# Ending a kernel in more and smaller output tiles: the third token tile in two parts, the fourth in three, stores on two queues in turn

## The chip, the cores and the metric

The kernel runs on one core of one Trainium2 chip. Its time is device time in microseconds (us). Every execution quoted here was in the fast state, with TensorE's granted clock at 1.0 (0.999 in one of e7's). A comparison counts as faster or slower only when it is clear of 2%, which is 32 us here.

TensorE (PE) multiplies matrices, VectorE (DVE) does the additions, ScalarE (ACT) and SyncE (SP) issue the stores, and 16 DMA engines move the data. Engines and DMAs tell each other that something is done by counters called semaphores, and an instruction can wait for them. An accumulator is what the matmuls of one part write (`dacc` and `dacc_pair` in the traces), called a bank; in the code below `pair` is one tile made of two of them.

## The reference

```python
x = x + A(layernorm(x), wqkv, wo)                # attention over 8 positions, 2 apart
x = x + B(layernorm(x), W_gate, W_up, W_down)    # h = relu(x @ W_gate) * (x @ W_up); h @ W_down
x = x + A(layernorm(x), wqkv, wo)
x = x + B(layernorm(x), W_gate, W_up, W_down)
# x: 2048 tokens x 1024 columns, bf16; hidden width 3584
```

The change concerns only the last thing that the kernel does: the product with `W_down` for the last block of 512 tokens, for the second half (512) of the 1024 columns. Its result is added to x and stored. The 512 tokens are four tiles of 128, called t0 to t3 below. The hidden width gives 28 contraction steps of 128.

## The kernel before

```python
def cols_of(half):                               # the parts in which a half is accumulated
    cols = [(t, 0, SLAB) for t in range(TPB)]    # four token tiles, 512 columns each
    if n == NN - 1 and half == 1:                # the very last half: t3 in two parts
        cols[-1:] = [(TPB - 1, 0, SLAB // 2), (TPB - 1, SLAB // 2, SLAB)]
    return cols

def mults(half, s8):                             # 8 of the 28 steps (4 in the last call)
    ...
    if half == 1:
        pair = psum_l.tile([P, TPB // 2, BLK], F32, tag="L", name="dacc_pair")   # two banks, one tile
        own = {2: pair[:, 0, :], 3: pair[:, 1, :]} if len(cols) == TPB else {2: pair[:, 0, :]}
    accs[half] = [own[i] if i in own else psum.tile([P, BLK], F32, tag="acc", ...)[:] for i in range(len(cols))]
    ...
    for a, (t, c0, c1) in zip(accs[half], cols):
        for jl in range(nfc):
            mm(a[:, c0:c1], lhsT=hT[:, j, t * P:(t + 1) * P], rhs=wsl[:, jl, c0:c1], ...)

def adds(half):
    for a, (t, c0, c1) in zip(accs[half], cols_of(half)):
        run(nc.vector.tensor_tensor, xs, a[:, c0:c1], xs, op=ALU.add)
        if n == NN - 1:
            if half == 1 and t % 2 == 1 and c0 == 0:
                nc.scalar.dma_start(dst, xs)     # ScalarE's queue
            else:
                sp_dma(dst, xs)                  # SyncE's queue
...
def store_x(n):                                  # stores of the three blocks ahead of the last
    for t in range((n % NB) * TPB, (n % NB + 1) * TPB):
        sp_dma(out_dram[t * P:(t + 1) * P, :], x_tiles[t][:])
```

An output part goes through four steps: its matmuls in the four last steps of the contraction, its addition on VectorE, the issue of its store, the store's landing. After that come SyncE's five closing waits, each for two semaphores.

## Time and profile before

| | before |
|---|---|
| time, median of 3 runs | 1618.47 us (1617.82 to 1618.52) |
| span of the profiled run | 1616.7 us |
| PE busy | 1611.1 us |
| last matmul ends / last add ends | 1613.57 / 1614.09 us |
| last store issued / landed | 1614.12 / 1615.68 us |

The page's engines and its chain that ended last (each step followed back to what released it) of the kernel before:

```profile
PE 1611.1 (100%) x7633; PEld 786.4 (49%) x7633; DVE 1137.4 (70%) x960; ACT 475.5 (29%) x967; POOL 180.9 (11%) x168
PE 99%; DMA 1%; DVE 0%; POOL 0%; issue 0%; DVEq 0%
```

TensorE has no slack, so the rest of the kernel can't hide anything for the end. What can be gained lies behind the last matmul.

The timeline of that end, kernel before. The columns are start in us, length in us, engine, line, operation, what it writes and reads, and, in brackets, idle time before it and what ended it. SPq and ACTq are issues of DMAs by those engines:

```profile
1611.01 0.69 DVE L831 TENSOR_TENSOR x<-dacc,x 128x512 bf16<-128x512 f32 x1 [20.95 <-PE dacc L132]
1611.67 1.03 PE L132 MATMUL dacc_pair<-w_d,hT 128*128 128x512 bf16 x4
1611.73 2.72 SPq L121 DMA_DIRECT2D out_dram<-x  x3
1611.87 0.69 DVE L831 TENSOR_TENSOR x<-dacc,x 128x512 bf16<-128x512 f32 x1 [0.17 <-PE dacc L132]
1612.54 1.04 PE L132 MATMUL dacc<-w_d,hT 128*128 128x256 bf16 x8
1612.60 1.55 ACTq L841 DMA_DIRECT2D out_dram<-x  x2
1612.74 0.69 DVE L831 TENSOR_TENSOR x<-dacc_pair,x 128x512 bf16<-128x512 f32 x1 [0.17 <-PE dacc_pair L132]
1613.34 0.75 DVE L831 TENSOR_TENSOR x<-dacc,x 128x256 bf16<-128x256 f32 x2
```

Each of the adds of t0, t1 and t2 waits for TensorE. The two adds of t3 follow without a wait, so VectorE sets the end there.

The same place one block earlier, kernel before, where t2 and t3 use both banks of the pair (timeline of VectorE):

```profile
1465.91 0.69 DVE L831 TENSOR_TENSOR x<-dacc,x 128x512 bf16<-128x512 f32 x1 [20.89 <-PE dacc L132]
1466.77 0.69 DVE L831 TENSOR_TENSOR x<-dacc,x 128x512 bf16<-128x512 f32 x1 [0.17 <-PE dacc L132]
1468.50 1.29 DVE L831 TENSOR_TENSOR x<-dacc_pair,x 128x512 bf16<-128x512 f32 x2 [1.04 <-PE dacc_pair L132]
```

Here VectorE sits idle for 1.04 us, until the matmuls of *both* banks are done, and then adds both at once. So here the two accumulators of one tile are released together.

### The profile page before, as it was taken

To read this page: it belongs to the slowest core of one execution; us is meant where nothing else is said; L and a number is where in the kernel's file an instruction comes from. 1 tells how busy PE (TensorE), PEld (TensorE's weight loads), DVE (VectorE), ACT (ScalarE), POOL (GpSimd) and SP (SyncE) were. 2 spreads that over 40 slices of the span, in tenths; PEclk is the share of its full clock that TensorE was granted. 3 is DMA by queue.
4 is the path that set the end of the run, shared out by engine and by line. 5 is a ranking of instruction groups with operands and counts; after the bars stand their busy time and mean duration, and the time that the engine had idled before them with its cause. 6 is when DMAs were issued, how large, how long until landed. Compare 5 with 4: busy or idle time off the path is not lost.

```text
span 1616.7 us, 18929 instructions
## 1 busy us (share of the span) xinstructions
PE 1611.1 (100%) x7633; PEld 786.4 (49%) x7633; DVE 1137.4 (70%) x960; ACT 475.5 (29%) x967; POOL 180.9 (11%) x168
## 2 busy tenths in 40 slices
PE   9999999999999999999999999999999999999999
PEld 6646544444444445444454444544445444444444
DVE  5999979996989698929489293893939939311211
ACT  5753312131116313603136031360313311131110
POOL 2400100010003002300053000530005100000000
PEclk9999999999999999999999999999999999999999
DMA  9868868697669766794747947479574884755452
GB/s 302 186 187 242 222 158 261 183 215 204 209 190 220 199 183 213 191 247 149 223 159 204 239 152 228 154 202 256 160 230 153 209 240 156 209 161 177 157 167 67
DMA packets 407448, 317.92 MB, mean 197 GB/s; under 512 B 166464, under 2 KB 387008, under 8 KB 406848
## 3 DMA queue, kind: packets, MB, share of 16 engines
q1 hardware_dynamic: 406784, 316.13, 69.5%
q8 instruction: 59, 0.97, 0.2%
q10 hardware_dynamic: 576, 0.59, 0.1%
q14 instruction: 29, 0.24, 0.0%
HBM read 266.29 MB, written 34.66 MB: 186 GB/s over the span
## 4 chain that ended last, share of the span: by engine, by line
PE 99%; DMA 1%; DVE 0%; POOL 0%; issue 0%; DVEq 0%
PE acc_u L132 24%; PE acc_g L132 24%; PE dacc L132 18%; PE acc_wo L132 7%; PE acc_q L132 7%; PE acc_k L132 7%; PE acc_v L132 7%; PE dacc_pair L132 6%; DMA w_u<-in_B_W_up_dram 0%; DMA x<-in_A_x_dram 0%; POOL rstd L328 0%; DVE xn_first L106 0%; DVE bst L106 0%; PE tp_pair L383 0%; DVE bst L103 0%
## 5 line engine op out<-in xcount | busy, mean ns | idle before, releaser
L132 PE MATMUL acc_u<-xnT_b,w_u 128*128 128x512 bf16 x1792 | 423.3, 379 | 0.1
L132 PE MATMUL acc_g<-xnT_b,w_g 128*128 128x512 bf16 x1792 | 423.3, 379 | 0.0
L784 ACT ACTIVATE r<-acc_g 128x512 bf16<-128x512 f32 x224 | 133.6, 596 | 725.4 <-PE acc_g L132 699.4
L106 DVE TENSOR_TENSOR hT<-acc_u,r 128x512 bf16<-128x512 f32 x224 | 151.3, 690 | 240.6 <-PE acc_u L132 238.2
L132 PE MATMUL dacc<-w_d,hT 128*128 128x512 bf16 (+1 forms) x1400 | 301.9, 375 | 0.0
L132 PEld LDWEIGHTS <-hT 128*128 128x128 bf16 x1820 | 178.1, 98 | 209.0
L132 PEld LDWEIGHTS <-w_u 128*128 128x128 bf16 x1792 | 175.3, 98 | 211.7 <-DMA w_u<-in_B_W_up_dram 0.6
L132 PEld LDWEIGHTS <-w_g 128*128 128x128 bf16 x1792 | 175.3, 98 | 211.4
L106 DVE TENSOR_TENSOR pv<-a,vhm 128x4096 bf16<-128x4096 bf16 x64 | 143.7, 2290 | 0.0
L831 DVE TENSOR_TENSOR x<-dacc,x 128x512 bf16<-128x512 f32 (+1 forms) x38 | 24.5, 673 | 154.1 <-PE dacc L132 154.1
L602 DVE TENSOR_TENSOR t<-q,k 128x2048 f32<-128x2048 bf16 x56 | 128.1, 2293 | 6.7 <-ACT k L537 4.6
L106 DVE TENSOR_TENSOR t<-q,k 128x2048 f32<-128x2048 bf16 x56 | 127.6, 2290 | 3.7 <-ACT k L537 2.6
L106 DVE TENSOR_TENSOR pv<-pv 128x1024 bf16<-128x1024 bf16 (+1 forms) x128 | 113.9, 957 | 0.0
L543 POOL COPY kh<-k 128x14 bf16<-128x14 bf16 x40 | 56.0, 1405 | 504.4 <-ACT k L537 504.4
L132 PE MATMUL acc_wo<-w_o,oT 128*128 128x512 bf16 x512 | 112.0, 379 | 0.0
L615 DVE TENSOR_TENSOR ac<-ac,t 128x2048 f32<-128x2048 f32 x48 | 109.7, 2286 | 0.3
L106 DVE TENSOR_TENSOR ac<-ac,t 128x2048 f32<-128x2048 f32 x48 | 109.8, 2288 | 0.0
L264 POOL TENSOR_TENSOR st_b<-st_b,neg_half 128x1 f32<-128x1 f32 x29 | 43.9, 1521 | 526.2 <-ACT st_b L263 526.2
L132 PE MATMUL dacc_pair<-w_d,hT 128*128 128x512 bf16 x420 | 95.9, 379 | 0.0
L132 PEld LDWEIGHTS <-oT 128*128 128x128 bf16 x512 | 50.1, 98 | 60.6 <-DMA w_o<-in_A_wo_dram 0.5
L259 ACT ACTIVATE xn_b<-x 128x1024 bf16<-128x1024 bf16 x29 | 30.3, 1045 | 128.4 <-DVE x L106 66.3
L441 ACT CAST vT<-acc_v 128x512 bf16<-128x512 f32 x56 | 32.7, 586 | 57.7 <-PE acc_v L132 56.7
(134 smaller groups left out, 1230.1 us busy)
## 6 DMA issues: line engine op xcount, KB each, us to landing
w_g<-in_B_W_gate_dram SPq DMA_DIRECT2D x56, 1024.0 KB, 7.2
w_u<-in_B_W_up_dram SPq DMA_DIRECT2D x56, 1024.0 KB, 5.3
w_d<-in_B_W_down_dram SPq DMA_DIRECT2D x48, 1024.0 KB, 5.7
w_o<-in_A_wo_dram SPq DMA_DIRECT2D x16, 1024.0 KB, 7.1
vhm<-v_d SPq DMA_DIRECT2D x32, 284.0 KB, 6.8
v_d<-vT SPq DMA_DIRECT2D x8, 1024.0 KB, 9.6
oT<-o_d SPq DMA_DIRECT2D x32, 256.0 KB, 4.0
w_d<-in_B_W_down_dram SPq DMA_DIRECT2D x16, 512.0 KB, 3.8
```

The costliest lines, as they stand in the source:

```text
L106: tail_dve[0] = f(*args, **kwargs).ins
L132: tail_pe[0] = nc.tensor.matmul(*args, **kwargs).ins
L259: nc.scalar.activation(xn, xt[:], ACT.Square, accum_out=sq)
L264: nc.gpsimd.tensor_tensor(rstd, vpe, neg_half[:, 0:1], op=ALU.pow)
L441: tail_act[0] = nc.scalar.copy(st["vT"][:, c, :], acc[:]).ins
L543: nc.gpsimd.tensor_copy(khalo[n][:, c, :], k[:, BLK:BLK + HALO])
L602: nc.vector.tensor_tensor(t[:], i0, i1, op=ALU.mult)
L615: nc.vector.tensor_tensor(o, ac[:], t[:], op=ALU.add)
L784: tail_act[0] = nc.scalar.activation(rs[j][:], acc[:], ACT.Relu).ins
L831: run = dv if n < NB - 2 else (lambda f, *args, **kwargs: f(*args, **kwargs))
```

## The change

The intent: a smaller last part is added and stored sooner, so less work is left when TensorE stops. t2 is cut into 256 and 256 columns, t3 into 256, 128 and 128. The seven stores alternate between the two queues so that the last one is on SyncE.

```diff
-                cols[-1:] = [(TPB - 1, 0, SLAB // 2), (TPB - 1, SLAB // 2, SLAB)]
+                cuts = [0, SLAB // 2, 3 * SLAB // 4, SLAB]
+                cols[-2:] = ([(TPB - 2, 0, SLAB // 2), (TPB - 2, SLAB // 2, SLAB)] +
+                             [(TPB - 1, c0, c1) for c0, c1 in zip(cuts, cuts[1:])])
...
-                        own = {2: pair[:, 0, :], 3: pair[:, 1, :]} if len(cols) == TPB else {2: pair[:, 0, :]}
+                        own = {2: pair[:, 0, :], 3: pair[:, 1, :]}
...
+                stores = []
...
-                        if half == 1 and t % 2 == 1 and c0 == 0:
-                            nc.scalar.dma_start(dst, xs)
-                        else:
-                            sp_dma(dst, xs)
+                        stores.append((dst, xs))
+                    if stores and half == 0:
+                        sp_dma(*stores.pop())
+                for i, (dst, xs) in enumerate(stores):
+                    if (len(stores) - i) % 2 == 0:
+                        nc.scalar.dma_start(dst, xs)
+                    else:
+                        sp_dma(dst, xs)
```

With the new list of parts, `pair[:, 0]` and `pair[:, 1]` hold the two parts of t2.

## The prediction

> **What bounds the kernel now.** TensorE: the chain that ended last is 99% PE; the page gives PE 1611.1 us busy of a 1616.7 us span at full clock. The change touches only the end of the last stage, so only the tail can change. In the timeline there (us from the span's start) the token tiles' last matmuls end at 1610.97 (t0), 1611.84 (t1), 1612.70 (t2), 1613.14 and 1613.57 (halves of t3). VectorE adds start at 1611.01, 1611.87, 1612.74, 1613.34, 1613.68; the last ends at 1614.09. Its store is issued on SP at 1614.12 and lands at 1615.68 (1.57 us); closing waits take 0.9 us. After t2 the adds follow at VectorE's own pace.
>
> **Added.**
> 1. Matmuls. Start to start the trace has 215.8 ns for 512 columns, 109.2 for 256, 55.9 for 128 (in the first value product, also with new weights each time). [...] Splitting t2 adds 2 x 109.2 - 215.8 = 2.6 ns, splitting t3's second half 2 x 55.9 - 109.2 = 2.6 ns, at each of 28 contraction steps: 0.15 us, all critical. TensorE ends near 1613.72.
> 2. Adds. Start to start 608 ns for 512 columns, 332 for 256, about 194 for 128 (estimate). After t1: 3 x 332 + 2 x 194 = 1384 ns instead of 608 + 2 x 332 = 1272.
> 3. A wait for the shared pair. t2's halves sit in the two banks of one pair tile. Where both banks are used in earlier blocks, the first one's add waits for the second one's matmuls (block before: pair's first add at 1468.50, as t3 ends at 1468.46). So t2's first half, done near 1612.40, waits for the second, near 1612.84: VectorE starts at 1612.87, not 1612.61. That cancels what splitting t2 could give.
>
> **Removed.** The last add shrinks from 415 to about 280 ns (estimate), the last store from 64 to 32 KB: eight packets per DMA engine, of 27 ns at 512 B in the tail, 18 ns at 256 B elsewhere: about 0.07 us. Alternating queues saves nothing: the last three stores alternated already.
>
> **Sum.** Adds start at 1612.87, 1613.20 (t2), 1613.54, 1613.87, 1614.06 (t3); the last ends near 1614.35 against 1614.09. Its store lands near 1614.38 + 1.50 = 1615.88 against 1615.68. Net +0.2 us, below the run to run spread (0.7 us). Without the pair wait the last add would end near 1614.12 and the result would be about -0.05 us.
>
> Prediction: 1618.7 us, 8 in 10 within 1617.7 to 1619.7. Faster by over 2%: 0.005; within 2%: 0.99; slower by over 2%: 0.005.
>
> **What would show it.** Matmul starts 109 and 56 ns apart in the last half; TensorE ends 0.15 us later; t2's first half is added only after its second is done; last add ends 0.2 to 0.3 us later; last store lands within 1.6 us of its issue; closing unchanged.
>
> **What would make it wrong.** The pair waits by bank after all (0.25 us less); 256-byte rows store slower than 512-byte ones [...]; a reorder of adds or stores; a wait for a free accumulator at the start of the last half (five of six instead of four; the earlier ones are added by 1590.1, before TensorE needs them, so I expect none); a shift of all runs between sessions.

The sum came to +0.26 us to the end of the last add (0.15 of it matmuls), less 0.07 us for the smaller store, which is +0.2 us. The 2.6 ns for each split follow from the three measured spacings. The two estimates for 128 columns agree with half the step from 512 to 256 columns (332 - 276/2 = 194 ns start to start, 415 - 277/2 = 277 ns long); the changed kernel's trace has 198 and 279 ns.

## More of the kernel before

The DMA view of the last microseconds, kernel before (times issued, KB each, median us from issue to landing):

```profile
out_dram<-x SPq DMA_DIRECT2D x2, 128.0 KB, 1.7
out_dram<-x ACTq DMA_DIRECT2D x1, 128.0 KB, 1.7
out_dram<-x ACTq DMA_DIRECT2D x1, 64.0 KB, 1.6
out_dram<-x SPq DMA_DIRECT2D x1, 64.0 KB, 1.6
```

## The result, and the profile after

| | before | after |
|---|---|---|
| median of 6 runs | 1618.49 us (1617.82 to 1618.82) | 1619.66 us (1618.97 to 1620.20) |
| mean of 6 runs | 1618.42 us | 1619.59 us |
| ratio of the fast runs | | 1.0007 (95%: 0.9994 to 1.002) |

A ratio is the mean time of one kernel's fast runs over that of the other's in the same rounds, so it isn't quite the ratio of the medians. The two sets of runs don't overlap, and the difference of the means, +1.17 us, is six times the +0.2 us forecast. The median lies inside the predicted range, 0.04 us from its edge, and three of the six runs lie outside.

The timeline of the end, changed kernel:

```profile
1611.54 0.69 DVE L833 TENSOR_TENSOR x<-dacc,x 128x512 bf16<-128x512 f32 x1 [21.07 <-PE dacc L132]
1612.20 1.04 PE L132 MATMUL dacc_pair<-w_d,hT 128*128 128x256 bf16 x8
1612.26 3.20 SPq L121 DMA_DIRECT2D out_dram<-x  x4
1612.40 0.69 DVE L833 TENSOR_TENSOR x<-dacc,x 128x512 bf16<-128x512 f32 x1 [0.17 <-PE dacc L132]
1613.07 1.05 PE L132 MATMUL dacc<-w_d,hT 128*128 128x256 bf16 x12
1613.12 1.80 ACTq L848 DMA_DIRECT2D out_dram<-x  x3
1613.27 0.76 DVE L833 TENSOR_TENSOR x<-dacc_pair,x 128x256 bf16<-128x256 f32 x2 [0.18 <-PE dacc_pair L132]
1613.94 0.81 DVE L833 TENSOR_TENSOR x<-dacc,x 128x256 bf16<-128x256 f32 x3
```

All of it lies later because this execution lost about 0.4 us well before the end (the add that closes the first half starts at 1589.77 instead of 1589.37). The change doesn't reach back that far, and e1 below, the same kernel again, has this add at 1589.20. So below all times of the end are taken from that add: the start of VectorE's add of t3 in the *first* half. The line at 1613.27 shows the predicted pair wait: both parts of t2 are added together.

The last issues in their own window, before:

```profile
1613.79 0.35 ACTq L841 DMA_DIRECT2D out_dram<-x  x1
1614.12 0.33 SPq L121 DMA_DIRECT2D out_dram<-x  x1
```

and after:

```profile
1614.47 0.28 DVE L833 TENSOR_TENSOR x<-dacc,x 128x128 bf16<-128x128 f32 x1
1614.59 0.34 ACTq L848 DMA_DIRECT2D out_dram<-x  x1
1615.12 0.33 SPq L121 DMA_DIRECT2D out_dram<-x  x1
```

The last add ends at 1614.47 + 0.28 = 1614.75, and the last store is issued only at 1615.12: 0.37 us later. Before it was 0.03 us. And it lands late, as the DMA view of the end shows, changed kernel:

```profile
out_dram<-x SPq DMA_DIRECT2D x1, 128.0 KB, 1.7
out_dram<-x ACTq DMA_DIRECT2D x1, 128.0 KB, 1.7
out_dram<-x SPq DMA_DIRECT2D x2, 64.0 KB, 1.6
out_dram<-x ACTq DMA_DIRECT2D x1, 64.0 KB, 1.6
out_dram<-x ACTq DMA_DIRECT2D x1, 32.0 KB, 1.6
out_dram<-x SPq DMA_DIRECT2D x1, 32.0 KB, 2.1
```

Two stores have 32 KB. The one on ACT takes 1.6 us, the last one, on SP, 2.1 us.

Taken apart, from the trace's records (us; the first row counts from the add that closes the first half, and each row below starts where the one above ended):

| step | before | after | difference |
|---|---|---|---|
| to the end of the last matmul | 24.207 | 24.346 | +0.139 |
| to the end of the last add | 0.518 | 0.634 | +0.116 |
| to the issue of the last store | 0.027 | 0.369 | +0.342 |
| to its landing | 1.566 | 2.065 | +0.499 |
| to the end of the span | 0.972 | 1.095 | +0.123 |
| sum | 27.290 | 28.509 | +1.219 |

The sum agrees with the clock's +1.17 us. The first two rows are the prediction's: 0.15 of matmuls and 0.26 to the end of the last add (measured 0.139 + 0.116 = 0.255). The other three, 0.96 us, it had put at -0.07.

A look at SyncE's own records shows what stands in the gap. They are counted from 0 (SyncE's instructions as the trace lists them, its waits for semaphores included):

```
 SyncE record             before                          after
 845  store issued        1614.118-1614.451 (the last)    1614.386-1614.718
 846  wait                1614.495-1614.522 closing       1614.763-1614.780
      no wait, nothing    0.357 us                        0.342 us
 847                      1614.879 closing wait           1615.122 the last store
 instruction packet       1615.629, 8192 B, 0.471 us      1616.015, 8192 B, 0.421 us
```

In both kernels SyncE pauses for 0.34 to 0.36 us in front of record 847, and 1.1 to 1.2 us after the pause begins, an 8 KB packet of the kind that the profile labels "instruction" occupies one DMA engine for over 0.4 us (0.471 and 0.421). In the kernel before record 847 is a closing wait, behind the last issue, where SyncE would wait for the landing anyway. The changed kernel issues one store more on SyncE, with one wait of its own, which is two records more, and so record 847 *is* the last store. The wait ahead of it, record 846, isn't what holds it up: the DMA that it asks for had landed at 1592.49. The store's packets lie between 1616.0 and 1616.2, but for eight of the 128, one engine's share: those come at 1616.4 to 1616.5, behind the instruction packet, which ends at 1616.436.

The pause is periodic. Records 207, 335, 719 and 847 have it bare (0.342 to 0.364 us in the two traces); 79, 463 and 591 are the other records at the same spacing of 128, where waits of 1.1 to 6.5 us would cover it. Between one of these seven records and the next lie 72 to 82 issues of DMAs, so the spacing is one of records and not of issues. What SyncE does in the pause and what the packet carries no trace shows.

### The profile page after: what moved, and what is told of

It reads as the page before. It is cut to its first block, busy times and chain, and to the rows that moved or that the text cites. A ratio compares the mean times of both kernels' runs of the same rounds, so it can differ in the third digit from the quotient of the medians.

```text
span 1618.3 us, 19047 instructions
## 1 busy us (share of the span) xinstructions
PE 1611.2 (100%) x7689; PEld 789.8 (49%) x7689; DVE 1137.2 (70%) x962; ACT 475.6 (29%) x967; POOL 180.3 (11%) x168
## 4 chain that ended last, share of the span: by engine, by line
PE 98%; DMA 1%; DVE 0%; POOL 0%; issue 0%; ACT 0%; SPq 0%; DVEq 0%; ACTq 0%
PE acc_u L132 24%; PE acc_g L132 24%; PE dacc L132 18%; PE acc_q L132 7%; PE acc_v L132 7%; PE acc_wo L132 7%; PE acc_k L132 6%; PE dacc_pair L132 6%; DMA w_o<-in_A_wo_dram 1%; DMA x<-in_A_x_dram 0%; POOL rstd L328 0%; DVE xn_first L106 0%; DVE bst L106 0%; DVE x L833 0%; PE tp_pair L383 0%
## 5 line engine op out<-in xcount | busy, mean ns | idle before, releaser
L132 PE MATMUL dacc<-w_d,hT 128*128 128x512 bf16 (+2 forms) x1428 | 302.0, 371 | 0.0
L833 DVE TENSOR_TENSOR x<-dacc,x 128x512 bf16<-128x512 f32 (+2 forms) x39 | 24.5, 658 | 154.3 <-PE dacc L132 154.3
L132 PE MATMUL dacc_pair<-w_d,hT 128*128 128x512 bf16 (+1 forms) x448 | 95.9, 366 | 0.0
```

The source lines that it names most:

```text
L132: tail_pe[0] = nc.tensor.matmul(*args, **kwargs).ins
L833: run = dv if n < NB - 2 else (lambda f, *args, **kwargs: f(*args, **kwargs))
```

## The experiments

The theory (R): the pause stands in front of SyncE's record 847 whatever the program does there, the 8 KB packet follows it, and the surprise of the change is where that record falls. Its rivals: rows of 256 bytes store slowly by themselves (S); more stores on two queues hold each other up (Q). To move record 847 without touching the end, earlier output stores are each issued as two halves, with k of them halved:

```diff
 def store_x(n):
     for t in range((n % NB) * TPB, (n % NB + 1) * TPB):
+        if (n - NN + NB) * TPB + t % TPB < k:
+            sp_dma(out_dram[t * P:(t + 1) * P, 0:SLAB], x_tiles[t][:, 0:SLAB])
+            sp_dma(out_dram[t * P:(t + 1) * P, SLAB:D], x_tiles[t][:, SLAB:D])
+            continue
         sp_dma(out_dram[t * P:(t + 1) * P, :], x_tiles[t][:])
```

All twelve runs gave the correct result. By the clock all are "same" at 2%, with 95% intervals of the ratio that hold 1. "Clock" is the mean of 5 runs less the mean of before's 9 runs of the same call. "End" is the span from the add that closes the first half to the end, in the profile, less before's 27.290; the columns ahead of it are the table's steps (us). Each end is that of one trace; the three kernels that were traced twice differ from themselves by 0.12 us (changed, e1), 0.03 (e10, e11) and 0.01 (e8, e12):

| run | record 847 is | matmul | add | issue | landing | closing | end | clock |
|---|---|---|---|---|---|---|---|---|
| before | a closing wait | 24.207 | 0.518 | 0.027 | 1.566 | 0.972 | | |
| e1 changed, again | the last store | 24.344 | 0.639 | 0.367 | 2.194 | 1.085 | +1.34 | +1.22 |
| e2 changed, k=3 | the wait after t0's store | 24.344 | 0.639 | 0.062 | 1.569 | 0.974 | +0.30 | +0.16 |
| e3 before, k=1 | the last store | 24.206 | 0.517 | 0.106 | 2.089 | 1.016 | +0.64 | +0.74 |
| e4 as e2, t2's parts apart | the wait after t0's store | 24.345 | 0.413 | 0.062 | 1.545 | 0.972 | +0.05 | +0.14 |
| e5 t2 in two only | second closing wait | 24.275 | 0.584 | 0.027 | 1.562 | 1.048 | +0.21 | +0.11 |
| e6 t3 in three only | second closing wait | 24.275 | 0.573 | 0.069 | 1.596 | 1.055 | +0.28 | +0.13 |
| e7 changed, k=1 | store of t3's first part | 24.346 | 0.637 | 0.157 | 1.848 | 1.111 | +0.81 | +1.08 |
| e8 before, k=7 | far ahead of the end | 24.205 | 0.519 | 0.026 | 1.603 | 0.839 | -0.10 | -0.16 |
| e9 changed, queues exchanged | second closing wait | 24.345 | 0.635 | 0.070 | 1.542 | 1.413 | +0.72 | +0.47 |
| e10 as e4, k=5 | far ahead of the end | 24.345 | 0.410 | 0.058 | 1.605 | 0.849 | -0.02 | -0.61 |
| e11 e10 again | far ahead of the end | 24.346 | 0.409 | 0.056 | 1.590 | 0.840 | -0.05 | -0.89 |
| e12 e8 again | far ahead of the end | 24.206 | 0.517 | 0.027 | 1.604 | 0.849 | -0.09 | -0.84 |

**e1, the changed kernel again.** No edit.

> The changed kernel again, beside the others. Theory R [...] its 848th instruction in the trace (ordinal 847, counted from 0) is always preceded by a pause of about 0.35 us, and some 1.2 us later an 8 KB instruction packet holds one DMA engine for 0.4 us. In the changed kernel that instruction is the last store's issue. Expected again: issue of the last store 0.37 us after the last add, landing about 2.06 us after issue, whole kernel +1.2 us against before (0.8 to 1.6). Rival S (small rows): 256-byte rows land slowly by themselves. Rival Q (queues): seven stores on two queues hold each other up. R, S and Q all expect the same of this run; it is the yardstick.

"Its 848th instruction" is SyncE's.

It did it again: issue 0.37 us after the add, landing 2.19 us after the issue. The instruction packet took 0.836 us this time, twice as long as in the first profile. The last store in the DMA view of the end, e1:

```profile
out_dram<-x SPq DMA_DIRECT2D x1, 32.0 KB, 2.2
```

**e2, the changed kernel with three earlier stores halved** (k=3).

> The changed kernel, with three output stores of earlier blocks each issued as two halves, so that SyncE has about six more instructions before the tail and the pause falls before the first of the last stores, where SyncE waits 20 us anyway. The tail's own stores are untouched. Theory R: the last store is issued within 0.05 us of the last add's end, lands 1.5 to 1.65 us after it, and the kernel is 0.7 to 1.1 us faster than the changed one, +0.1 to +0.5 us against before. S and Q: nothing changes, last landing still about 2.06 us after issue, +1.2 us against before.

The seven stores, their sizes and their queues are those of e1, and the surprise is gone: 1.339 - 0.298 = 1.04 us by the end's trace, 1.06 us by the clock. The store is issued 0.062 us after the add, a little over the 0.05 expected, as it follows right behind SyncE's store before. The DMA view of the end, e2:

```profile
out_dram<-x SPq DMA_DIRECT2D x1, 128.0 KB, 1.7
out_dram<-x ACTq DMA_DIRECT2D x1, 128.0 KB, 2.1
out_dram<-x SPq DMA_DIRECT2D x2, 64.0 KB, 1.6
out_dram<-x ACTq DMA_DIRECT2D x1, 64.0 KB, 1.6
out_dram<-x ACTq DMA_DIRECT2D x1, 32.0 KB, 1.6
out_dram<-x SPq DMA_DIRECT2D x1, 32.0 KB, 1.6
```

The last store is back at 1.6 us. The late landing has moved to t1's store on ACT (2.1 us instead of 1.7), which isn't the last and costs nothing: the instruction packet now comes 0.54 us before the last matmul ends. S and Q, which expected no change, fall as explanations of the surprise.

**e3, the kernel before with one earlier store halved** (k=1).

> The kernel before, with one earlier output store issued as two halves: about two more SyncE instructions before the tail, tail itself unchanged. Theory R: the pause now falls before the last store. SyncE is ready there 0.27 us before the add ends, so the issue comes only about 0.1 us late; but the instruction packet should be in the DMA engines with that store's packets, landing 1.9 to 2.1 us after issue instead of 1.57; and one more closing wait comes after it (0.07 us). Sum +0.3 to +0.7 us against before. S and Q: no 256-byte rows and no more stores on two queues at the end, so 0.0 us.

The kernel before, without any of the change, gets the same fault. Its DMA view of the end, e3, to be held against before's:

```profile
out_dram<-x SPq DMA_DIRECT2D x2, 128.0 KB, 1.7
out_dram<-x ACTq DMA_DIRECT2D x1, 128.0 KB, 1.7
out_dram<-x ACTq DMA_DIRECT2D x1, 64.0 KB, 1.7
out_dram<-x SPq DMA_DIRECT2D x1, 64.0 KB, 2.1
```

The pause itself costs only 0.08 us here (0.106 - 0.027), because SyncE is idle before this store and pauses while the add still runs (the store before is issued by 1613.47, the add ends at 1613.77). The landing carries the rest, 0.52 us. By the clock it was +0.74 us, just over the +0.7 that was the top of what was expected.

How much of the late landing are the held packets? In e3 the last store's last packet ends 0.51 us later after the issue than in before, in e1 0.54: nearly all of the 0.52 and 0.63 us. In the first profile of the changed kernel it is only 0.24 of the 0.50 us. The rest falls between the last packet and the landing, and stays open.

**e4, e2 with the parts of t2 in different tiles.** `pair` keeps one bank in use, as in the kernel before:

```diff
-                        own = {2: pair[:, 0, :], 3: pair[:, 1, :]}
+                        own = {2: pair[:, 0, :], 3: pair[:, 1, :]} if len(cols) == TPB else {2: pair[:, 0, :]}
```

> As the changed kernel with three halved earlier stores, and besides the second half of the third tile accumulates in a bank of its own instead of the second bank of the pair. Theory P (pair wait, as predicted): the first half's add starts about 0.26 us earlier, as soon as VectorE is free after t1's add, and the last add ends about 0.23 us earlier, so 0.2 us faster than the run with the pair, about +0.05 us against before. Rival: VectorE's pace alone sets the end of the last add, and the pair wait is hidden: 0.0 us.

The timeline of VectorE from t1's add on, e2:

```profile
1611.58 0.69 DVE L833 TENSOR_TENSOR x<-dacc,x 128x512 bf16<-128x512 f32 x1 [0.17 <-PE dacc L132]
1612.45 0.76 DVE L833 TENSOR_TENSOR x<-dacc_pair,x 128x256 bf16<-128x256 f32 x2 [0.18 <-PE dacc_pair L132]
1613.12 0.81 DVE L833 TENSOR_TENSOR x<-dacc,x 128x256 bf16<-128x256 f32 x3
```

and e4:

```profile
1612.56 0.69 DVE L833 TENSOR_TENSOR x<-dacc,x 128x512 bf16<-128x512 f32 x1 [0.17 <-PE dacc L132]
1613.16 0.41 DVE L833 TENSOR_TENSOR x<-dacc_pair,x 128x256 bf16<-128x256 f32 x1
1613.49 1.19 DVE L833 TENSOR_TENSOR x<-dacc,x 128x256 bf16<-128x256 f32 x4
```

In e4 the first part's add follows t1's add 0.61 us after that one's start instead of 0.87 (1612.56 to 1613.16, against 1611.58 to 1612.45), with no wait, and the last add ends 0.639 - 0.413 = 0.226 us earlier, as forecast (0.23). The clock can't see it (1618.61 against 1618.63 us). The pair wait is real and worth 0.23 us.

**e5 and e6, one part of the change alone.** e5 keeps t3 in two parts:

```diff
-                cuts = [0, SLAB // 2, 3 * SLAB // 4, SLAB]
+                cuts = [0, SLAB // 2, SLAB]
```

e6 leaves t2 whole, and uses the pair as e4 does:

```diff
-                cols[-2:] = ([(TPB - 2, 0, SLAB // 2), (TPB - 2, SLAB // 2, SLAB)] +
+                cols[-1:] = (
                              [(TPB - 1, c0, c1) for c0, c1 in zip(cuts, cuts[1:])])
```

> Only the third tile in two parts (both banks of the pair); the fourth stays in two parts of 256. Six stores, so SyncE issues three of them as in before and its pause (instruction 847) falls behind the last issue. Theory R plus the predicted terms: matmuls +0.07 us, last add ends about 0.06 us later after the last matmul (the first half waits for the second), one closing wait more: +0.2 us against before (0.0 to 0.4), last store landing 1.55 to 1.65 us after issue. If instead the parts of the change add up plainly, this part or the next has to carry most of the 1.2 us.

> Only the fourth tile in 256, 128 and 128 columns; the third whole. Six stores, three on SyncE. Theory R plus the predicted terms: +0.2 us against before (0.0 to 0.4), last store (256-byte rows) landing 1.5 to 1.6 us after issue. Rival S (256-byte rows land slowly): landing about 2.1 us, +0.7 us or more. Both parts together by R: 0.4 us; whole change: 1.2 us; the rest is the fourth store on SyncE.

Each alone costs 0.21 and 0.28 us at the end, together 0.48 us; the whole change costs 1.2 to 1.3. The parts don't add up, because each alone leaves SyncE with three stores and record 847 behind them. e6 has the 256-byte rows as its last store, and they land in 1.596 us, against 1.566 for the 512-byte rows of before.

**e7, the changed kernel with one earlier store halved** (k=1).

> The changed kernel with one earlier store halved: the pause moves one store forward, before the store of the fourth tile's first part, where SyncE has 0.27 us to spare. Theory R: that store is issued about 0.08 us late and the last one right behind it, within 0.2 us of the last add; the instruction packet meets earlier stores; the last store lands 1.55 to 1.8 us after issue; +0.4 to +0.8 us against before, so 0.5 to 0.9 us better than the changed kernel. Rival: halving any earlier store helps by itself, however many: then it would be as fast as with three halved stores (+0.2 us).

Record 847 is now the store before the last on SyncE. Issue and landing both recover only in part. The landing takes 1.848 us, above the 1.8 that was the top of what was expected. The instruction packet starts 1.044 us after the last matmul, and the last three stores, on both queues, all take 1.85 to 1.99 us. So here several stores behind the packet are late, not one; why all of them are isn't shown. By the end's trace this is 0.5 us better than the changed kernel, by the clock only 0.1 us (+1.08, where +0.4 to +0.8 was expected); the five runs spread from 1618.71 to 1619.93 us, and the profile is that of the fastest. That halving any earlier store helps by itself, the rival, doesn't fit either: the end is 0.51 us longer than with three halved.

**e9, the changed kernel with its queues exchanged.** The test in the loop of the stores is turned round, so ScalarE issues four, the last among them:

```diff
-                    if (len(stores) - i) % 2 == 0:
+                    if (len(stores) - i) % 2 == 1:
```

> The changed kernel with the two queues exchanged for its last seven stores: ScalarE issues four, the last among them, SyncE three. Nothing earlier is touched. Theory R: SyncE's instruction 847 is now its second closing wait, and its first closing wait is the one for the last store, so the pause of 0.35 us comes bare after the last landing and its packet too late to meet a store. Expected: last store issued within 0.05 us of the last add, landing 1.5 to 1.65 us after issue, then a gap of 0.35 us between first and second closing wait; tail from the last matmul to the end about 3.6 us (before 3.08, changed kernel 4.1 to 4.3); +0.5 to +0.9 us against before. Rival Q (stores on two queues hold each other up): landing still about 2.1 us, no gap after it, +1.2 us. Rival: the number of stores on SyncE alone matters, not which instruction meets the pause: +0.2 us as with six stores.

This takes the pause and the packet apart. The last store lands 1.542 us after its issue, since the packet is too late to meet it (it starts 1.0 us after the landing). The line in the DMA view, e9:

```profile
out_dram<-x ACTq DMA_DIRECT2D x1, 32.0 KB, 1.5
```

But SyncE's first closing wait is the one for this store, and the pause comes bare behind it, from the records of SyncE:

```
 845  store of t3's second part   0.463 to 0.795 us after the last matmul
 846  first closing wait          ends 2.270 (last landing 2.247)
      no wait, nothing            0.337 us
 847  second closing wait         2.607
```

So the closing takes 1.413 us, about 0.33 more than the 1.085 of e1, which has the same waits behind its landing. The pause by itself is worth 0.34 us at the end. The end came out at 3.66 us after the last matmul (24.345 + 3.660 = 28.005), where 3.6 was expected. By the clock it was +0.47 us, just under the range of +0.5 to +0.9 us; by the mean span of the program's instructions +0.80 (on this difference see e10). The rival by which only the number of stores on SyncE matters, three here as in e5 and e6, expected +0.2.

**e8 and e12, the kernel before with seven earlier stores halved** (k=7).

> The kernel before with seven earlier stores halved. The pause falls well before the tail, and the eight semaphores that stores take in turn move on by seven, so that the last store's semaphore is in the last of the five closing waits and not in the third: two waits of about 0.067 us less after the last landing. Expected: tail after the last matmul 0.13 us shorter, kernel 0.13 us faster than before (-0.4 to +0.2 by the clock, too small for the timing; the trace decides). Rival: the closing waits cost nothing, 0.0 us.

> The kernel before with seven earlier stores halved, once more, as the other candidate: tail 2.99 us from the last matmul as in its first run, -0.1 us against before, -0.4 to +0.2 by the clock.

The closing shrinks from 0.972 to 0.839 and 0.849 us: the last store's semaphore is in the last of the five closing waits and not in the third. This also accounts for the +0.123 us in the changed kernel, where it is in the first and four waits follow its landing. By e8 one such wait is worth about 0.067 us, half of 0.972 - 0.839. The end is 0.10 and 0.09 us shorter, where 0.13 was expected: the landing takes 0.04 us longer.

**e10 and e11, a try for the best.** e4 with k=5 instead of 3.

> A try for the best of all: the changed kernel, third tile's halves in banks of different tiles, and five earlier stores halved, so that the pause falls before the tail and the last store's semaphore is in the last of the five closing waits. Expected: tail from the last matmul to the end 2.86 us (2.99 with three halved, less two waits of 0.067), with 0.15 us more of matmuls: -0.08 us against before (-0.4 to +0.3 by the clock). If the prediction's 0.15 us of matmuls or the pair wait were wrong, it would come out above +0.1 us or below -0.2 us in the trace.

> The run before once more: it came out 0.61 us faster than before by the clock, while its tail (2.92 us from the last matmul, plus 0.15 us of matmuls, against 3.08) explains 0.01 us. If the 0.6 us are noise of executions, the difference is now between -0.4 and +0.3 us with the same tail; if they are real, it is -0.4 to -0.8 us again and something ahead of the tail must be shorter.

The end is 0.02 and 0.05 us shorter than before's. By the clock the two runs are 0.61 and 0.89 us faster, and e12 0.84, all three outside what was expected. The larger part lies outside the program. The clock mostly reads 1.7 us more than the span from the first to the last instruction, but in several of before's runs in these two calls 2 to 3.9 us more; the run at 1620.36 has a span of only 1616.5. By the mean spans e10 is 0.24, e11 0.34 and e12 0.36 us shorter than before. Their ends explain 0.02 to 0.09 us of that; the rest stays unexplained. All intervals hold 1. So no version here beats both kernels beyond doubt. By the traces the kernel before with k=7 and the changed kernel with k=5 and no shared pair come to within 0.1 us of each other and of before.

## Why the prediction was right or wrong

The forecast of "within 2%", and that nothing would be gained, was right. The size, +0.2 us, was wrong by 1.0 us. That the median still fell inside the range is luck: the terms that failed add up to 0.96 us, and the range ends 1.0 us above the forecast. Point by point:

- **"Splitting t2 adds 2 x 109.2 - 215.8 = 2.6 ns ... 0.15 us, all critical."** Right: 0.139 us to the end of the last matmul, 0.068 in each of e5 and e6, where one split is made. 0.139 us over 56 more matmuls is 2.5 ns each.
- **"A wait for the shared pair ... cancels what splitting t2 could give."** Right, and shown by taking it away: 0.226 us (e4 against e2). But without the pair wait, and with the pause out of the way, the end is still 0.05 us longer than before (e4), where the prediction had "about -0.05 us". The shorter last add (0.413 against 0.518 us after the last matmul) is worth less than the added matmuls.
- **"The last ends near 1614.35 against 1614.09."** Right: 0.255 us later, by the table of steps.
- **"About 0.07 us" less for a 32 KB store.** Not found in the landing. Undisturbed, the last 32 KB landed in 1.542 to 1.605 us (e2, e4, e6, e9 to e11), the last 64 KB in 1.562 to 1.604 (before, e5, e8, e12). At this size neither a penalty nor a gain showed in the landing. The packets did what was forecast: 18 ns for 256 bytes and 27 for 512 in the tail (46 for 1024, so 14, 19 and 22 bytes per ns: the smaller the slower), and from the last store's first packet to the end of its last 0.26 to 0.27 us in these six runs instead of 0.36. But the first packet came 0.06 to 0.09 us later after the issue, and in five of the six the landing 0.02 to 0.07 us later after the last packet.
- **"Alternating queues saves nothing."** Right as to saving. But the step missed that the choice of queue decides how many instructions SyncE has to issue.
- **"Last store lands within 1.6 us of its issue; closing unchanged", with "its store lands near 1614.38 + 1.50".** This is the step that failed. The sum carried the issue, landing and closing of before over as constants. They were constants of *that* instruction stream: SyncE's pause at record 847 was hidden behind the last issue. One store more brought it in front of the last one: issue +0.342 us, landing +0.499, closing +0.123 because the store's semaphore moved to the first closing wait. e2 takes the first two away without touching the end, e3 puts them into the kernel before, e9 shows the pause without the packet, e8 and e12 show the closing waits.

What SyncE does in the pause stays open. What the runs show is that it keeps its record number in every kernel built here in which no longer wait covers it (0.337 to 0.368 us), and that the packet follows it wherever it overlapped the end. It also stays open why three runs have spans 0.2 to 0.3 us shorter than their traces' ends explain.

## What to carry to other kernels

Cutting the last tile finer pays only as long as the shorter add and store exceed the time that the extra matmuls add over the whole contraction: here 56 of them added 0.139 us, and the last add then ended 0.105 us sooner after the last matmul (0.413 us in e4 against 0.518). Give parts that are to be released one by one a tile each: the two that shared one were released together, at 0.226 us (e2 against e4). At the scale of a microsecond the end of a kernel can depend on where the issuing engine's instruction count stands, as it did here for SyncE (1.04 us between e1 and e2): look for a gap without a wait in front of the last issue, and if there is one, move it by adding, removing or redistributing earlier DMA issues, not by changing the end. Compare such changes by the stretch of trace that they touch, from an event just ahead of it, because a whole execution can shift by more than was forecast for the change: two traces of the changed kernel had the add that closes the first half at 1589.77 and at 1589.20, 0.57 us apart, against +0.2 us.
